# State products of an attention block on quarters and column halves of the array, with compact state and two result banks

## The chip, the cores and the metric

One core of a Trainium2 chip. The metric is the device time of one execution in microseconds, lower is better. All arithmetic is fp32.

## The reference

Attention with decay, in blocks along the sequence, and a mixture of experts on its result:

```python
for b in range(nb):
    intra = einsum('bhic,bhjc->bhij', qb, kb) * Dmask
    intra = einsum('bhij,bhjd->bhid', intra, vb)
    inter = einsum('bhid,bhde->bhie', qb * lam_pow, kv_state)     # query side of the state
    out[:, :, sl] = intra + inter
    kv_state = lam_block * kv_state + einsum('bhsd,bhse->bhde', kb * rev_pow, vb)   # state update
...
for e in range(E):
    out += p[:, e:e+1] * (maximum(x @ w1[e], 0) @ w2[e])
```

There are 4 batches, 8 heads of 64, 768 positions; then 3072 rows of 512 through 4 experts of width 1024. The kernel cuts the attention into 24 chunks of 128 positions, six per batch. The first chunk of a batch has no state to query, the last need not update it. Chunks 0 to 7 run in an opening of some 60 us, the others are strewn among the expert products, which take nearly all the time.

## The kernel before

Heads go in pairs (2hp, 2hp+1), one in each half of the 128 partitions. The state `kv` of a pair is a 128x128 block with two 64x64 blocks on its diagonal and zeros beside them. `half[0]` and `half[1]` are the two halves of the partitions.

```python
def values(n, tags):
    op = bank(tags[0], "op")
    if not first:
        for hp in range(NHP):                       # query side: 4 matmuls on the whole array
            nc.tensor.matmul(out=op[:, hp * C:(hp + 1) * C], lhsT=kv[:, hp], rhs=hc(qs)[:, hp],
                             start=(hp == 0), stop=False, skip_group_check=True)
    for hp in range(NHP):
        for hd in range(2):                         # scores times v: 8 matmuls on column halves
            nc.tensor.matmul(out=op[half[hd], hp * C:(hp + 1) * C], lhsT=vn[:, 2 * hp + hd], ...)
    nc.scalar.copy(out=xT[:, :, c * C:(c + 1) * C], in_=hc(op))
    if not last:
        kp = bank(tags[1], "kvp")
        for hp in range(NHP):                       # state update: 4 matmuls on the whole array
            nc.tensor.matmul(out=hc(kp)[:, hp], lhsT=kn[:, 2 * hp:2 * hp + 2] ..., rhs=vn[:, 2 * hp:2 * hp + 2] ...)
        # later, on VectorE, for each half sl: kv[sl, :, sl] = kv[sl, :, sl] * decay + kpv[sl, :, sl]
```

The score products (64 rows of the contraction, two row halves) are a step of their own, `scores`. Between the steps run `pg` products (first layer, L549 here and L555 after) and `q` products (second layer, L601 and L607).

## Time and profile before

| | before |
|---|---|
| time, median of 4 runs | 1240.24 us (1239.68 to 1241.35) |
| span of the profiled run | 1241.5 us |
| TensorE busy | 1225.3 us |
| VectorE busy | 761.6 us |
| query side and state update, busy | 21.2 and 23.2 us |

TensorE is the bound and the products to be changed are a small part of it. The prediction shows the lines and how they are read. The spacing of starts is the cost of a matmul, not the duration in its row. And a gap of TensorE is printed at the instruction behind it, with what ended it.

### The profile page before, as it was taken

The numbers are of one execution on the slowest core, as the hardware profiler recorded it, in microseconds if no ns is written. First come the engines' busy times: TensorE is split into PE (matmuls) and PEld (weight loads), VectorE is DVE, ScalarE is ACT, GpSimd is POOL, SyncE is SP. The second block draws the span as 40 slices with busy tenths as digits, with TensorE's granted clock in tenths as the row PEclk, the third lists the DMA queues.
The fourth block names the chain that finished last, engine by engine and source line by source line (L and its number), as shares of the span: only waits on it lengthen the run. The fifth ranks groups of instructions, "written<-read, shape, count | busy, mean of one in ns | idle before, by whom it ended". The sixth has DMA issues, their size and how long they took to land.

```text
span 1241.5 us, 16264 instructions
## 1 busy us (share of the span) xinstructions
PE 1225.3 (99%) x6376; PEld 1074.6 (87%) x6376; DVE 761.6 (61%) x1268; ACT 216.9 (17%) x361; POOL 309.1 (25%) x314
## 2 busy tenths in 40 slices
PE   8999999999999999999999999999999999999998
PEld 6888887888888888888888888888888888888887
DVE  5586576577466846745664774764765755755742
ACT  2222111112212211221121120120120220220100
POOL 4520256672382865120000800000110000000001
PEclk9999999999999999999999999999999999999999
DMA  9652679999899699766544864545555454454422
GB/s 226 166 179 86 219 256 347 357 337 312 295 334 323 219 351 354 246 216 208 178 153 153 302 227 168 214 153 217 203 194 216 153 199 183 161 220 154 169 69 84
DMA packets 173277, 273.11 MB, mean 220 GB/s; under 512 B 87440, under 2 KB 120848, under 8 KB 173200
## 3 DMA queue, kind: packets, MB, share of 16 engines
q1 hardware_dynamic: 144384, 212.89, 50.8%
q10 hardware_dynamic: 26704, 53.41, 11.3%
q0 software_dynamic: 2112, 5.77, 1.2%
q8 instruction: 50, 0.82, 0.3%
q14 instruction: 27, 0.22, 0.0%
HBM read 212.39 MB, written 59.64 MB: 219 GB/s over the span
## 4 chain that ended last, share of the span: by engine, by line
PE 90%; DMA 3%; POOL 3%; DVE 2%; issue 0%; ACT 0%; SPq 0%; POOLq 0%; ACTq 0%; DVEq 0%
PE q L601 43%; PE pg L549 34%; PE pM L650 5%; PE sp L378 2%; PE op L405 2%; POOL ops L93 2%; PE kvp L414 2%; PE op L399 1%; DMA w_ops<-ops 1%; PE qp L355 1%; PE kp L355 1%; DMA w2b<-in_moe_w_dram 1%; DVE hS L93 1%; POOL w2o L93 1%; POOL w1o L93 1%; DVE m L93 1%
## 5 line engine op out<-in xcount | busy, mean ns | idle before, releaser
L549 PE MATMUL pg<-xs_in,ws_in 128*128 128x256 f32 x1960 | 472.1, 381 | 3.6 <-ACT m L557 2.5
L549 PEld LDWEIGHTS pg<-xs_in,ws_in 128*128 128x128 f32 x1960 | 371.5, 191 | 55.1 <-ACT m L557 2.9
L601 PE MATMUL q<-w2t,hS 128*128 128x256 f32 x1536 | 361.0, 380 | 0.0
L93 DVE TENSOR_TENSOR m<-pg,m 128x512 f32<-128x512 f32 x410 | 280.2, 689 | 107.2 <-PE pg L549 94.2
L601 PEld LDWEIGHTS q<-w2t,hS 128*128 128x128 f32 x1536 | 291.8, 190 | 39.2
L617 DVE SCALAR_TENSOR_TENSOR acc<-q,gate,acc 128x256 f32<-128x256 f32 x288 | 139.1, 483 | 247.8 <-PE q L601 247.5
L601 PE MATMUL q<-w2t,m 128*128 128x256 f32 x1152 | 270.7, 380 | 0.0
L601 PEld LDWEIGHTS q<-w2t,m 128*128 128x128 f32 x1152 | 219.1, 191 | 29.4
L620 POOL DMA_DIRECT2D out_dram<-acc x44 | 24.1, 548 | 545.9 <-DVE acc L617 545.9
L561 ACT ACTIVATE m<-m 128x512 f32<-128x512 f32 x120 | 75.5, 630 | 357.8 <-DVE m L93 347.2
L93 DVE TENSOR_TENSOR hS<-m,m 128x512 f32<-128x512 f32 x96 | 73.3, 768 | 13.2 <-ACT m L561 13.2
L557 ACT COPY m<-pg 128x512 f32<-128x512 f32 x80 | 46.8, 585 | 170.8 <-PE pg L549 164.3
L93 DVE TENSOR_TENSOR m<-m,m 128x512 f32<-128x512 f32 x96 | 70.5, 739 | 0.0
L503 ACT ACTIVATE m<-m 128x512 f32<-128x512 f32 x48 | 30.3, 630 | 148.7 <-DVE m L93 135.7
L93 POOL TENSOR_TENSOR kn<-kn,s_decay 128x256 f32<-128x256 f32 x40 | 28.2, 724 | 107.7 <-PE kp L355 94.4
L614 DVE TENSOR_SCALAR acc<-q,gate 128x256 f32<-128x256 f32 x48 | 23.2, 482 | 40.5 <-PE q L601 40.4
L650 PE MATMUL pM<-xt,w1o 128*128 128x256 f32 x192 | 43.9, 381 | 1.4 <-DVE xt L93 0.9
L650 PEld LDWEIGHTS pM<-xt,w1o 128*128 128x128 f32 x192 | 36.2, 190 | 7.0 <-DVE xt L93 1.3
L93 DVE TENSOR_TENSOR m<-pM,m 128x512 f32<-128x512 f32 x40 | 27.4, 688 | 22.6 <-PE pM L650 22.4
L93 DVE TENSOR_TENSOR hS<-hS,m 128x512 f32<-128x512 f32 x48 | 35.8, 746 | 0.3
L93 DVE TENSOR_TENSOR st<-sp,s_decay 128x512 f32<-128x512 f32 x48 | 32.1, 682 | 6.2 <-PE sp L378 6.1
L93 POOL TENSOR_TENSOR w2o<-w2b 128x1024 f32<-128x1024 f32 x8 | 19.0, 2379 | 67.8 <-DMA w2b<-in_moe_w_dram 42.2
(65 smaller groups left out, 778.1 us busy)
## 6 DMA issues: line engine op xcount, KB each, us to landing
xs_in<-x_ops SPq DMA_DIRECT2D x70, 896.0 KB, 4.7
ws_in<-w_ops SPq DMA_DIRECT2D x70, 896.0 KB, 6.5
w2t<-w_sums SPq DMA_DIRECT2D x96, 256.0 KB, 6.3
w2t<-in_moe_w_dram SPq DMA_DIRECT2D x72, 256.0 KB, 6.4
w_ops<-ops ACTq DMA_DIRECT2D x28, 512.0 KB, 6.3
x_ops<-ops ACTq DMA_DIRECT2D x21, 512.0 KB, 5.0
w2b<-in_moe_w_dram SPq DMA_DIRECT2D x32, 256.0 KB, 4.8
w_sums<-w2o ACTq DMA_DIRECT2D x16, 512.0 KB, 4.4
```

The lines of the kernel that those rows point to most:

```text
L93: eng.tensor_tensor(out=o, in0=a, in1=b, op=op)
L355: nc.tensor.transpose(out=x[:, hp * C:(hp + 1) * C], in_=y[:, 2 * hp:2 * hp + 2].rearrange("p h d -> p (h d)"), identity=ident[:],)
L378: nc.tensor.matmul(out=sp[hd][:, hp * C:(hp + 1) * C], lhsT=hc(kT)[half[hd], hp], rhs=hc(qT)[half[hd], hp], start=True, stop=True,)
L405: nc.tensor.matmul(out=op[half[hd], hp * C:(hp + 1) * C], lhsT=vn[:, 2 * hp + hd], rhs=hc(st[hd])[:, hp], start=(first and hp == 0), stop= ...
L414: nc.tensor.matmul(out=kpv[:, hp], lhsT=kn[:, 2 * hp:2 * hp + 2].rearrange("p h d -> p (h d)"), rhs=vn[:, 2 * hp:2 * hp + 2].rearrange("p ...
L503: nc.scalar.activation(out=o[:], in_=o[:], func=AF.Relu)
L549: nc.tensor.matmul(out=p[:, j * 256:(j + 1) * 256], lhsT=ws[:, W1_AT[i], j * P:(j + 1) * P], rhs=xs[:, X_AT[i]], start=(fresh and j == 0), ...
L557: nc.scalar.copy(out=new[at][:], in_=p[:])
L561: nc.scalar.activation(out=new[at][:], in_=new[at][:], func=AF.Relu)
L601: nc.tensor.matmul(out=p[:, s * DH:(s + 1) * DH], lhsT=h[A_OF[m]][:, c * 256 + s * P:c * 256 + (s + 1) * P], rhs=fed2[g, e, m][uu][:, c], ...
L617: nc.vector.scalar_tensor_tensor(out=o, in0=x, scalar=w, in1=o, op0=ALU.mult, op1=ALU.add)
L650: nc.tensor.matmul(out=p[:, s * 256:(s + 1) * 256], lhsT=a[c][:, f:f + P], rhs=b[:, c, j * 256:(j + 1) * 256], start=(s == 0 and c == 0), ...
```

## The change

Its intent: multiply no zeros and compute nothing that is thrown away. On the query side each head's 64x64 product takes one quarter of the array, four heads at once. In the state update all 128 positions are summed over, so each head takes a column half (128 rows, 64 columns), two heads at once. For the quarters a head needs its row half and its column half chosen separately. Heads are now numbered 4r + 2a + x: `r` is the half of the rows (and the result bank), `x` the half of the columns. The order of heads in memory changes for q and k, so these come in two loads each. The state is compact, 64 wide. The core of the diff:

```diff
-    op = bank(tags[0], "op")
+    op = [bank(tags[r], "op") for r in range(2)]
+    heads = [(a, r, c) for a in range(2) for r in range(2) for c in range(2)]
     if not first:
-        for hp in range(NHP):
-            matmul(out=op[:, hp * C:(hp + 1) * C], lhsT=kv[:, hp], rhs=hc(qs)[:, hp], ...)
+        for a, r, x in heads:
+            matmul(out=op[r][half[x], a * C:(a + 1) * C], lhsT=kv[half[r], 2 * a + x],
+                   rhs=hc(qs)[half[r], 2 * a + x], start=(a == 0), ...)
 ...
-    kp = bank(tags[1], "kvp")
-    for hp in range(NHP):
-        matmul(out=kpv[:, hp], lhsT=<pair of kn, 128 columns>, rhs=<pair of vn, 128 columns>, ...)
+    kvp = op[1][:, 2 * C:]                      # in the free half of a result bank
+    for ac in range(NHP):
+        for r in range(2):
+            matmul(out=kvp[half[r], ac], lhsT=kn[:, 2 * ac + r], rhs=vn[:, 4 * r + ac], ...)
 ...
-    nc.scalar.copy(out=xT[:, :, ...], in_=hc(op))
+    for r in range(2):
+        nc.scalar.copy(out=xT[:, 2 * r:2 * r + 2, ...], in_=op[r][:, 0:2 * C] ...)
 ...
-    # two halves: kv[sl, :, sl] = kv[sl, :, sl] * decay + kpv[sl, :, sl]
+    # one piece:  kv = kv * decay + kvp
 ...
-    nc.sync.dma_start(out=x, in_=src)                               # q, k: 256 KB
+    for r in range(2):
+        nc.sync.dma_start(out=to[:, :, r], in_=of[:, :, r])         # q, k: 2 x 128 KB
```

GpSimd's decay of k becomes one instruction instead of two.

More of the change, by code (lines that the diff above doesn't have):

```diff
@@ L100, in load @@
         for name in names:
-            x = small(f"{name}n")[:].rearrange("p (h d) -> p h d", d=D)
+            x = small(f"{name}n")
             src = {"q": q, "k": k, "v": v}[name][b, :, c * C:(c + 1) * C, :]
-            nc.sync.dma_start(out=x, in_=src.rearrange("h p d -> p h d"))
-            nat[n, name] = x
+            if name == "v":
+                nc.sync.dma_start(out=x[:].rearrange("p (h d) -> p h d", d=D), in_=src.rearrange("h p d -> p h d"))
+            else:
+                to, of = x[:].rearrange("p (i r d) -> p i r d", r=2, d=D), src.rearrange("(r i) p d -> p i r d", r=2)
+                for r in range(2):
+                    nc.sync.dma_start(out=to[:, :, r], in_=of[:, :, r])
+            nat[n, name] = x[:].rearrange("p (h d) -> p h d", d=D)
     lam_bc = consts.tile([P, H], FP32, name="lam_bc")
@@ L290 @@
     s_decay = consts.tile([P, 2, NHP, C], FP32, name="s_decay")
-    for hd in range(2):
-        for hp in range(NHP):
-            h = 2 * hp + hd
+    for r in range(2):
+        for ac in range(NHP):
+            h = 4 * r + ac
             nc.vector.tensor_tensor_scan(
-                out=s_decay[:, hd, hp], data0=lam_bc[:, h:h + 1].to_broadcast([P, C]), data1=ident[:],
+                out=s_decay[:, r, ac], data0=lam_bc[:, h:h + 1].to_broadcast([P, C]), data1=ident[:],
                 initial=0.0, op0=ALU.mult, op1=ALU.add,
@@ L302 @@
     q_decay = consts.tile([P, NHP, C], FP32, name="q_decay")
-    for hd in range(2):
-        nc.vector.tensor_copy(
-            out=q_decay[half[hd], :, 0], in_=lam_bc[half[hd], :].rearrange("p (hp hd) -> p hd hp", hd=2)[:, hd],
-        )
+    for r in range(2):
+        nc.vector.tensor_copy(out=q_decay[half[r], :, 0], in_=lam_bc[half[r], 4 * r:4 * r + 4])
     m = 1
@@ L313 @@
         m *= 2
-    kv = consts.tile([P, NHP, P], FP32, name="kv")
-    nc.vector.memset(kv[:], 0.0)
+    kv = consts.tile([P, NHP, D], FP32, name="kv")
     probs = consts.tile([P, NTOK // P, E], FP32, name="probs")
@@ L353, in turn @@
         for x, y in ((qp, qn), (kp, kn)):
-            for hp in range(NHP):
+            for ac in range(NHP):
                 nc.tensor.transpose(
-                    out=x[:, hp * C:(hp + 1) * C], in_=y[:, 2 * hp:2 * hp + 2].rearrange("p h d -> p (h d)"),
+                    out=x[:, ac * C:(ac + 1) * C], in_=y[:, 2 * ac:2 * ac + 2].rearrange("p r d -> p (r d)"),
                     identity=ident[:],
@@ L366, in turn @@
         if n % NCH < NCH - 1:
-            for hd in range(2):
-                kd = kn.rearrange("p (hp hd) d -> p hd hp d", hd=2)[:, hd]
-                tt(nc.gpsimd, kd, kd, k_decay[:, hd].unsqueeze(2).to_broadcast([P, NHP, D]), ALU.mult)
+            kd = kn.rearrange("p (ac r) d -> p ac r d", r=2)
+            by = k_decay.rearrange("p r ac -> p ac r").unsqueeze(3)
+            tt(nc.gpsimd, kd, kd, by.to_broadcast([P, NHP, 2, D]), ALU.mult)
     def scores(n, tags):
         qT, kT, _ = turned[n]
-        sp = [bank(tags[hd], "sp") for hd in range(2)]
-        for hp in range(NHP):
-            for hd in range(2):
+        sp = [bank(tags[r], "sp") for r in range(2)]
+        for ac in range(NHP):
+            for r in range(2):
                 nc.tensor.matmul(
-                    out=sp[hd][:, hp * C:(hp + 1) * C], lhsT=hc(kT)[half[hd], hp], rhs=hc(qT)[half[hd], hp],
+                    out=sp[r][:, ac * C:(ac + 1) * C], lhsT=hc(kT)[half[r], ac], rhs=hc(qT)[half[r], ac],
                     start=True, stop=True,
@@ L395, in values @@
         first, last = n % NCH == 0, n % NCH == NCH - 1
-        op = bank(tags[0], "op")
+        op = [bank(tags[r], "op") for r in range(2)]
+        heads = [(a, r, c) for a in range(2) for r in range(2) for c in range(2)]
         if not first:
-            for hp in range(NHP):
+            for a, r, x in heads:
                 nc.tensor.matmul(
-                    out=op[:, hp * C:(hp + 1) * C], lhsT=kv[:, hp], rhs=hc(qs)[:, hp], start=(hp == 0), stop=False,
-                    skip_group_check=True,
-                )
@@ L403, in values @@
-        for hp in range(NHP):
-            for hd in range(2):
-                nc.tensor.matmul(
-                    out=op[half[hd], hp * C:(hp + 1) * C], lhsT=vn[:, 2 * hp + hd], rhs=hc(st[hd])[:, hp],
-                    start=(first and hp == 0), stop=True, skip_group_check=True,
-                )
-        nc.scalar.copy(out=xT[:, :, c * C:(c + 1) * C], in_=hc(op))
-        if not last:
-            kp = bank(tags[1], "kvp")
-            kpv = hc(kp)
-            for hp in range(NHP):
-                nc.tensor.matmul(
-                    out=kpv[:, hp], lhsT=kn[:, 2 * hp:2 * hp + 2].rearrange("p h d -> p (h d)"),
-                    rhs=vn[:, 2 * hp:2 * hp + 2].rearrange("p h d -> p (h d)"), start=True, stop=True,
-                )
-            def state(sl):
+                    out=op[r][half[x], a * C:(a + 1) * C], lhsT=kv[half[r], 2 * a + x], rhs=hc(qs)[half[r], 2 * a + x],
@@ new lines, in values @@
+                    start=(a == 0), stop=False, skip_group_check=True,
+                )
+        for a, r, x in heads:
+            nc.tensor.matmul(
+                out=op[r][half[x], a * C:(a + 1) * C], lhsT=vn[:, 4 * r + 2 * a + x], rhs=hc(st[r])[:, 2 * a + x],
+                start=(first and a == 0), stop=True, skip_group_check=True,
+            )
+        kvp = op[1][:, 2 * C:].rearrange("p (h d) -> p h d", d=D)
+        if not last:
+            for ac in range(NHP):
+                for r in range(2):
+                    nc.tensor.matmul(
+                        out=kvp[half[r], ac], lhsT=kn[:, 2 * ac + r], rhs=vn[:, 4 * r + ac], start=(ac == 0), stop=True,
+                        skip_group_check=True,
+                    )
@@ L420, in state @@
+        for r in range(2):
+            nc.scalar.copy(
+                out=xT[:, 2 * r:2 * r + 2, c * C:(c + 1) * C],
+                in_=op[r][:, 0:2 * C].rearrange("p (a t) -> p a t", t=C),
+            )
+        if not last:
+            def state():
                 if first:
-                    nc.vector.tensor_copy(out=kv[sl, :, sl], in_=kpv[sl, :, sl])
+                    nc.vector.tensor_copy(out=kv[:], in_=kvp)
                 else:
-                    tt(
-                        nc.vector, kv[sl, :, sl], kv[sl, :, sl], q_decay[sl, :, C - 1:C].to_broadcast([D, NHP, D]),
-                        ALU.mult,
-                    )
@@ L427, in state @@
-                    tt(nc.vector, kv[sl, :, sl], kv[sl, :, sl], kpv[sl, :, sl], ALU.add)
-            soon(n, *(lambda sl=sl: state(sl) for sl in half))
+                    tt(nc.vector, kv[:], kv[:], q_decay[:, :, C - 1:C].to_broadcast([P, NHP, D]), ALU.mult)
+                    tt(nc.vector, kv[:], kv[:], kvp, ALU.add)
+            soon(n, state)
     def attention(g):
```

## The prediction

> **What bounds the kernel now.** I read the page first: the busy row and the chain that ended last.
>
> ```profile
> span 1241.5 us, 16264 instructions
> PE 1225.3 (99%) x6376; PEld 1074.6 (87%) x6376; DVE 761.6 (61%) x1268; ACT 216.9 (17%) x361; POOL 309.1 (25%) x314
> PE 90%; DMA 3%; POOL 3%; DVE 2%; issue 0%; ACT 0%; SPq 0%; POOLq 0%; ACTq 0%; DVEq 0%
> ```
>
> TensorE has work for 1225 of 1241 us, and 90% of the chain lies on it. A microsecond taken from TensorE comes off the span, except in the other 10%. The groups by shape then tell how much of it the change touches:
>
> ```profile
> L378 PE MATMUL sp<-qT,kT 64*128 64x128 f32 x384 | 29.7, 298 | 1.3 <-ACT kT L361 1.3
> L405 PE MATMUL op<-st,vn 128*64 128x128 f32 x384 | 26.6, 282 | 0.0
> L414 PE MATMUL kvp<-vn,kn 128*128 128x128 f32 x160 | 23.2, 288 | 0.0
> L399 PE MATMUL op<-qs,kv 128*128 128x128 f32 x160 | 21.2, 276 | 1.1 <-DVE kv L421 1.1
> ```
>
> The state products are L399 and L414, some 20 us each (the busy times include pipeline tails). "128*128" is the array tile: today both use the whole array, although half of what they multiply is zeros (L399) or thrown away (L414). That caps the gain: 40 of 1240 us, if they vanished. L378 and L405 already use halves ("64*128", "128*64"). A mean of 276 ns says little, as matmuls overlap, so I read cost as the distance between starts, from the timeline of TensorE around one chunk:
>
> ```profile
> 610.63 1.68 PE L549 MATMUL pg<-xs_in,ws_in 128*128 128x256 f32 x7
> 612.14 1.05 PE L399 MATMUL op<-qs,kv 128*128 128x128 f32 x8
> 613.12 1.09 PE L405 MATMUL op<-st,vn 128*64 128x128 f32 x16
> 614.15 1.16 PE L414 MATMUL kvp<-vn,kn 128*128 128x128 f32 x8
> 615.14 1.03 PE L601 MATMUL q<-w2t,hS 128*128 128x256 f32 x4
> ```
>
> An fp32 matmul of the program is two records, so x8 is four matmuls. L399 starts at 612.14, L601 at 615.14: the chunk's products take 3.00 us. Single records of 128 columns on the whole array start 0.110 us apart; 8 x 0.110 = 0.88, and L399 takes 0.98. L405 issues 16 records in 1.03: single records show them in pairs, two within 7 ns, pairs 0.110 apart, so the two halves run truly together. Sum: 3 x 0.88 = 2.64, and 0.36 for two changes of tile shape.
>
> Last, the chain between 122 and 220 us, the one long stretch not on TensorE:
>
> ```profile
> 141.48 4.06 DMA w_sums<-w2o
> ...
> 187.75 1.65 POOL kn L93 x2
> 189.40 1.83 POOL ops L93 x2
> ...
> 204.76 8.89 DMA w_ops<-ops
> ...
> 214.67 3.67 PE pg L549 x8
> ```
>
> From 126 to 214 us the weights' sums on GpSimd and their DMAs set the pace; TensorE ends by waiting 2.5 us for them.
>
> **What the Trainium skill says.** "TensorEngine Tiling (Array Packing)", Key Properties: tiles work independently, 64x64 gives four of them, and a change of tiling mode drains TensorE. The trace agrees for halves (pairs 7 ns apart) and shows the drain as the 0.36 us above. Gotcha 1: PSUM Pressure on that page: different row tiles must not use one PSUM bank at once; hence the two result banks here, one per row half. "TensorE: Matmul & The Clock Gate", LDWEIGHTS: load time goes with the columns of the stationary operand, P/1.2 ns; a 64-column load is half a 128-column one. Trace: 138 against 192 ns for the records, which include a fixed part. The same page, Back-to-back issue gap, gives a floor of about 25 ns between matmul starts, or 62 ns where the sequencer decodes in software. The trace has 7 ns inside a pair but never more than two per 110 ns, so it does not show whether four per 110 ns can be sustained.
>
> **The change part by part.**
>
> TensorE, query side (L399): 4 full matmuls become 8 of 64x64 (16 records), ordered so that four neighbours lie on four quarters. With four at once: 16/4 x 0.110 = 0.44 us, from 0.88. State update (L414): 4 full matmuls of 128 columns become 8 column-half matmuls of 64 columns: 8 pairs x 0.055 = 0.44, from 0.88. They use L405's shape and follow it, so that change of shape goes. L405's own work stays 0.88. Changes of shape: full to quarters 0.15, quarters to column halves 0.15, halves to full 0.20; 0.50, from 0.36. Middle chunk: 0.44 + 0.88 + 0.44 + 0.50 = 2.26, from 3.00: 0.74 saved. First chunk of a batch (no L399): 0.44. Last (no L414): 0.44 - 0.15 = 0.29.
>
> There are 24 chunks, 16 middle, 4 first, 4 last. If all counted: 11.8 + 1.8 + 1.2 = 14.8 us. Now where they lie:
>
> - Chunks 0 and 1 finish before the transposes of chunk 4. The load of k for chunk 4 was issued at 19.35 and took 7.4 us, so it landed at 26.75; its transpose ran at 26.90. DMA is above 90% busy there. Whatever is saved before (some 1.5 us) is swallowed by that landing.
> - Chunks 2 to 7: in this part a score product with row halves follows, so one shape change goes entirely and a middle chunk saves 0.93. Chunks 2 to 4: 2.8; chunk 5: 0.3; chunks 6 and 7, up to the first matmul that waits for VectorE at 65.66: about 2.0, since the state update before that wait is two VectorE instructions shorter. Sum 5.1.
> - Chunk 8 (168.8 us) lies inside the GpSimd and DMA chain: its 0.74 is absorbed.
> - Chunks 9 to 23, behind 214 us: 10 middle, 2 first, 3 last: 7.4 + 0.9 + 0.9 = 9.2.
>
> VectorE: the state is compact, 128x256 in place of two 64x256, so 72 instructions become 36. At 0.42 to 0.67 us each 18 us of 762 go. Worth time only where VectorE holds TensorE: before 417.7 and 424.8 us, idle 0.35 + 0.73 us, where the chain passes through four kv instructions (2.2 us). I count 1.0.
>
> ScalarE: the 24 result copies of 128x512 (584 ns) become 48 of 128x256, estimated 370 ns each (fixed part plus half the elements): 4 us more of 217, off the path. The kv update now waits for the second copy, as they share a bank; the background queue hides that after the opening, and in chunk 6 the single kv copy makes up for it. GpSimd: 40 decays of 128x256 become 20 of 128x512, about as long in all. DMA: q and k come in two halves; the runs stay 256 bytes, so packets and bytes stay, 48 issues more. First matmul perhaps 0.3 us later, hidden by the landing above; that landing may slip 0.5.
>
> Sum: 5.1 + 9.2 + 1.0 - 0.5 = 14.8, so 1240 - 15 = 1225 us.
>
> **The rivals.**
>
> (a) Quarters don't run four at once: the records of one fp32 matmul stand one behind the other in program order, and if TensorE looks only one tile ahead, or issue sustains only two starts per 110 ns, L399 stays 0.88 and the 64-column pairs take up to 0.88. Then only shape changes (+0.14 x 16) and VectorE remain: 1238 to 1242. For it: the trace has no denser issue. Against it: in the first 14 us, where all of TensorE's blocks take about twice as long (four transposes 1.09, later 0.60), 16 score records took 2.01 us (7.38 to 9.39), later 1.09; so the array sets that rate, not issue. And pairs start 7 ns apart although the second record of the first tile stands between them in program order. One of the two sides may fall alone: 1231 to 1234.
>
> (b) Supply takes the place: in 200 to 400 us DMA is 92 to 101% busy and the chain before 214 proves that feeding can bind. The tightest weight tile behind 214 landed 2.4 us before use, so a gain of 0.7 per chunk leaves it ahead. If the extra issues slow the queue: 1229 to 1234.
>
> (c) The opening becomes DMA-bound further, with twice as many q and k loads in the same eight rotating completion semaphores: up to 3 us of the 5.1 lost, 1228.
>
> (d) More than expected: wait chains through VectorE shorten elsewhere too, 1219 to 1221.
>
> **Range and chances.** The sum gives 1225, the rivals (b) and (c) pull up by a few us, (a) with perhaps a quarter of the chance by up to 15. Range 1218 to 1236. Faster by over 2% needs under 1215.3, a saving of 25 us, more than all state products could give at fourfold speed: 4%. Slower by over 2% needs 25 us lost on an engine that only gets less work: 2%. Within 2%: 94%.
>
> **What would show it.** Timeline of one middle chunk behind 214 us: query side about 0.59 us from start to start, L405's work 1.03, state update 0.6 to 0.7; the whole 2.2 to 2.3. Records in fours, 110 ns apart. If the query side shows about 1.0, rival (a) holds. The stall before the first product at 214.67 should become longer than 2.5 us by about 0.7, the idles near 417 and 425 should vanish, VectorE's busy time fall to about 744. TensorE idle in the opening near 26 us proves the k landing. The prediction is wrong in kind if TensorE's busy time does not fall by some 12 us, or if it falls and new waits of more than 5 us appear.

## The result, and the profile after

| | before | after |
|---|---|---|
| time, median of 4 runs | 1240.24 us | 1226.18 us (1224.29 to 1227.07) |
| span of the profiled run | 1241.5 | 1225.0 |
| TensorE busy | 1225.3 | 1209.3 |
| VectorE busy | 761.6 | 743.4 |
| ScalarE busy | 216.9 | 219.6 |

The ratio is 0.9884 (95%: 0.9866 to 0.9901). A ratio is the mean time of one kernel's runs over that of the other's of the same rounds, so not quite the ratio of the medians. It is a gain of 1.2%, inside the 2% that counts as the same.

The page of the changed kernel, busy row and chain:

```profile
PE 1209.3 (99%) x6696; PEld 1053.7 (86%) x6696; DVE 743.4 (61%) x1231; ACT 219.6 (18%) x385; POOL 305.5 (25%) x294
PE 92%; DMA 4%; POOL 2%; DVE 1%; ACT 0%; issue 0%; SPq 0%; POOLq 0%; DVEq 0%
```

TensorE issues 320 matmul records more and is busy 16 us less: more, smaller matmuls, several at once. The changed products in the groups by shape:

```profile
L405 PE MATMUL op<-qs,kv 64*64 64x128 f32 x320 | 13.3, 282 | 1.0 <-DVE kv L430 1.0
L418 PE MATMUL op<-vn,kn 128*64 128x64 f32 x320 | 12.7, 222 | 0.0
```

The mean of one query record has even risen, from 276 to 282 ns; the busy time fell from 21.2 to 13.3 us for twice as many. One middle chunk in TensorE's timeline (start, length, as before):

```profile
567.20 0.38 PE L555 MATMUL pg<-xs_in,ws_in 128*128 128x256 f32 x1
567.51 0.67 PE L405 MATMUL op<-qs,kv 64*64 64x128 f32 x16
568.11 1.09 PE L410 MATMUL op<-st,vn 128*64 128x128 f32 x16
569.03 0.64 PE L418 MATMUL op<-vn,kn 128*64 128x64 f32 x16
569.60 1.78 PE L607 MATMUL q<-w2t,hS 128*128 128x256 f32 x7
```

From 567.51 to 569.60 is 2.09 us, where the kernel before needed 3.00. That flatters: the record ahead, at 567.20, keeps TensorE 0.31 us where such a record else takes 0.216, and the first one behind takes 0.320. Part of the changes of shape is hidden in the neighbours. Counted from the last record ahead to the second one behind, less two ordinary ones, a middle chunk costs 3.44 - 0.43 = 3.01 us before and 2.72 - 0.43 = 2.28 after. Single records show the query side as four groups of four starts within 20 ns; the second group comes 160 ns after the first, the others 110 ns apart.

Where it went, by two landmarks that both timelines have. The first opening product (pM) that waits for VectorE started at 65.66 and now at 59.01, 6.65 us earlier; 0.70 of that is its shorter wait. The first product behind the wait for GpSimd and DMA started at 214.67 and now at 207.86, 6.81 earlier. The end came 16.5 earlier. So the opening gave 6.65 us, the stretch up to the wait 0.2, all behind it 9.7.

Before:

```profile
65.66 2.64 PE L650 MATMUL pM<-xt,w1o 128*128 128x256 f32 x11 [0.93 <-DVE xt L93]
214.67 1.65 PE L549 MATMUL pg<-xs_in,ws_in 128*128 128x256 f32 x3 [2.53 <-ACT m L557]
```

After:

```profile
59.01 9.30 PE L656 MATMUL pM<-xt,w1o 128*128 128x256 f32 x42 [0.23 <-DVE xt L93]
207.86 1.74 PE L555 MATMUL pg<-xs_in,ws_in 128*128 128x256 f32 x4 [3.23 <-ACT m L563]
```

The bracket is TensorE's idle time before the instruction: at the second landmark 3.23 us, 2.53 before the change.

### The profile page after: what moved, and what is told of

Read it like the earlier page. It is cut to its first block, busy times and chain, and to the rows that moved or that the text cites. A ratio compares the mean times of both kernels' runs of the same rounds, so it can differ in the third digit from the quotient of the medians.

```text
span 1225.0 us, 16958 instructions
## 1 busy us (share of the span) xinstructions
PE 1209.3 (99%) x6696; PEld 1053.7 (86%) x6696; DVE 743.4 (61%) x1231; ACT 219.6 (18%) x385; POOL 305.5 (25%) x294
## 4 chain that ended last, share of the span: by engine, by line
PE 92%; DMA 4%; POOL 2%; DVE 1%; ACT 0%; issue 0%; SPq 0%; POOLq 0%; DVEq 0%
PE q L607 44%; PE pg L555 34%; PE pM L656 5%; PE sp L382 2%; PE op L410 2%; PE kp L359 1%; PE op L405 1%; DMA w2t<-in_moe_w_dram 1%; PE qp L359 1%; POOL ops L93 1%; DMA w_ops<-w1b 1%; DMA w1b<-in_moe_w_dram 1%; PE op L418 1%; POOL w2o L93 1%; DVE hS L93 1%; DMA w_ops<-ops 0%
## 5 line engine op out<-in xcount | busy, mean ns | idle before, releaser
L93 DVE TENSOR_TENSOR hS<-m,m 128x512 f32<-128x512 f32 x96 | 67.5, 708 | 13.9 <-ACT m L567 13.9
L93 POOL TENSOR_TENSOR kn<-kn,s_decay 128x512 f32<-128x512 f32 x20 | 23.8, 1192 | 103.0 <-PE kp L359 100.8
L423 ACT COPY xT<-op 128x256 f32<-128x256 f32 x48 | 17.1, 373 | 118.6 <-PE op L410 90.9
```

Source lines behind the costliest of these rows:

```text
L93: eng.tensor_tensor(out=o, in0=a, in1=b, op=op)
```

## The experiments

**The state update alone.** Does each half pay by itself, and is it the array that pays? The kernel before, with the new state update only; pairs, loads and block-diagonal state as they were.

```diff
-    for hp in range(NHP):
-        matmul(out=kpv[:, hp], lhsT=<pair of kn>, rhs=<pair of vn>)
+    kpv = kp[:, 0:NHP * D]
+    for hp in range(NHP):
+        for hd in range(2):
+            matmul(out=kpv[half[hd], hp], lhsT=kn[:, 2 * hp + hd], rhs=vn[:, 2 * hp + hd], start=(hp == 0), ...)
```

> The kernel before with the state update alone changed: 8 column-half matmuls of 64 columns in place of 4 on the whole array; query side, loads and block-diagonal state as before. My theory (array time comes off the span): state update 0.56 us from start to start in place of 0.99, and about 0.43 less per chunk behind 214 us (12 chunks, 5.1 us) and 0.6 less in each of the seven of the opening (about 4): saves 8 to 9 us, 1231 to 1232. Rival (the gain of the whole change comes mainly from the shorter VectorE work and the opening's loads, which this run does not have): saves under 3 us, over 1237.

Measured: 1232.24 us, ratio 0.9930 (0.9909 to 0.9951). A chunk in its timeline:

```profile
569.39 1.05 PE L399 MATMUL op<-qs,kv 128*128 128x128 f32 x8
570.37 1.09 PE L405 MATMUL op<-st,vn 128*64 128x128 f32 x16
571.29 0.64 PE L415 MATMUL kvp<-vn,kn 128*64 128x64 f32 x16
571.86 0.91 PE L602 MATMUL q<-w2t,hS 128*128 128x256 f32 x3
```

The query side still takes 0.98 us, the state update 0.57 instead of 0.99, and the block ahead of it 0.92 instead of 1.02, since the shape no longer changes between them. 0.7% of 1240 is 8.7 us, as the theory had it. VectorE's work was not shortened here, so the rival falls.

**The query side alone.** The changed kernel with the state update back on the whole array.

```diff
-    for r in range(2):
-        matmul(out=kvp[half[r], ac], lhsT=kn[:, 2 * ac + r], rhs=vn[:, 4 * r + ac], ...)
+    matmul(out=kvp[ac // 2][:, ac % 2], lhsT=kn[:, 2 * ac:2 * ac + 2], rhs=<heads ac and 4 + ac of vn>, ...)
+    # VectorE reads the diagonal blocks in four pieces
```

> The changed kernel with the state update back on the whole array (4 matmuls of 128 columns, diagonal blocks read out by VectorE in four pieces): quarters for the query side alone. My theory: query block 0.60 us in place of 0.98, with 0.09 more on leaving the full array, so 0.29 less per chunk behind 214 us (13 chunks, 3.8 us) and 2.4 in the opening, state update back at 0.99: saves 5 to 7 us against the kernel before, 1233 to 1235. With the run of the state update alone the two savings should add up to the whole change's 14 to 16. Rival (quarters only pay together with the shared shape of the two column-half blocks): saves under 3.

Measured: 1236.04 us, ratio 0.9955 (0.9937 to 0.9973). By the ratio that is 5.6 us, within the 5 to 7; the time lies above the 1233 to 1235 expected. In its trace the query block takes 0.60 us and the state update 1.00, as before (0.99). By the ratios the two parts add to 8.7 + 5.6 = 14.3 us, and the whole change gives 0.0116 x 1240 = 14.4; that this agrees so well is partly luck, since each ratio is known to some 2.5 us. The traces are sharper. Compared with the kernel before, each chunk behind the wait at 214 us that has the product concerned saves 0.43 us in the first run and 0.29 in the second, and each of the ten that have both saves 0.72 in the changed kernel: block by block, the two parts add.

**The order of issue.** Does TensorE run four at once only because neighbours lie on different quarters?

```diff
-    for a, r, x in heads:
+    for a, r, x in sorted(heads, key=lambda t: (t[1], t[2], t[0])):
```

> The changed kernel with the query matmuls grouped by quarter (four records of one quarter in a row) in place of neighbours on four quarters. Theory A (TensorE starts what it finds for a free quarter anywhere in its queue): records still in fours, query block 0.60 us, time within 1 us of the changed kernel, 1226. Theory B (it looks past only a few waiting records, and the order of issue is what makes fours): fewer at once, query block 0.9 to 1.5 us, 20 chunks of which about 18 count, so 5 to 16 us slower, 1231 to 1242.

Measured: 1227.20 us, ratio 0.9886 (0.9869 to 0.9903). A chunk's query side and its successor:

```profile
569.97 0.69 PE L405 MATMUL op<-qs,kv 64*64 64x128 f32 x16
570.59 1.09 PE L410 MATMUL op<-st,vn 128*64 128x128 f32 x16
```

0.62 us from start to start, 0.02 more than before. Single records still start in fours, now 13 ns apart instead of 7, and the fours 110 ns apart. Four records of one quarter stand in a row in the program, so the first of the fourth quarter has to pass earlier ones that wait; TensorE lets it. (The trace doesn't name the quarter of a record. That each four is one of each quarter follows from the rate, and the spacing of 13 ns shows that the new order did reach TensorE.) Theory A holds, and my rival (a) falls with room to spare.

**The loads in halves.** The kernel before with q and k in two loads each.

```diff
-    nc.sync.dma_start(out=x, in_=src)
+    for hs in (slice(0, 4), slice(4, 8)):
+        nc.sync.dma_start(out=x[:, hs], in_=src[hs])
```

> The kernel before with q and k loaded in two halves each, as the changed kernel does, nothing else. My prediction let the landing of chunk 4's k (26.75 us) swallow what chunks 0 and 1 save; in the changed kernel it landed at 25.16. Theory A (smaller loads land earlier): here too it lands at 25 to 25.5, and the span stays within 2 us of before, since TensorE does not wait there. Theory B (it landed earlier because the changed kernel asks for it earlier, as TensorE frees things sooner): lands at 26.5 to 27 again.

Measured: 1241.08 us, ratio 1.0001 (0.9983 to 1.0018). Chunk 4's k landed at 25.57. Issued at 19.44 and 20.00, no earlier than the whole load of before (19.35), so it was not asked for earlier. From issue to landing a whole load took 7.4 us in two kernels (before and the state update alone), the second half 5.6 here and 4.8 to 5.4 in three others with halves. That speaks for theory A, though 25.57 lies just outside the 25 to 25.5 expected. Theory B isn't excluded as a second part: in the state update alone, with whole loads, k was issued at 18.39, 0.96 us earlier than before, and landed 0.95 earlier, at 25.80. It does not make the landing harmless. Where TensorE comes still earlier or the load later, it waits: in the state update alone 0.41 us for q and 0.27 for k; in the run with the other order of issue, where q landed at 25.43 and k at 26.32, like this:

```profile
25.56 0.63 PE L359 MATMUL qp<-ident,qn 128*128 128x128 f32 x4 [0.54 <-DMA qn<-in_q_dram]
26.41 0.63 PE L359 MATMUL kp<-ident,kn 128*128 128x128 f32 x4 [0.22 <-issue]
```

The changed kernel itself:

```profile
25.20 0.60 PE L359 MATMUL qp<-ident,qn 128*128 128x128 f32 x4
25.64 0.60 PE L359 MATMUL kp<-ident,kn 128*128 128x128 f32 x4
```

No bracket, so no wait. Nor is there one in its second profile. But of the six other profiles with the same code up to here (the two with padding, the two with pieces alone, and the two with the copies on VectorE) all show one, for q, k or both: 0.2 us in two of them, 0.6 to 1.7 in the other four. (I took two loads because versions with one load did not build with this order of heads; no run shows that.)

**Which chunks count.** The query products of one chunk done five times over: 4 x 0.44 us of added TensorE work with the same result, first in chunk 8, ahead of the wait at 208 us, then in chunk 13, behind it.

```diff
-    for a, r, x in heads:
+    for a, r, x in heads * (5 if n == 8 else 1):      # 13 in the second kernel
```

> The changed kernel with the query products of chunk 8 done five times over (same result): 4 x 0.44 = 1.8 us of added TensorE work inside the stretch before the stall at 208 us. My claim is that what chunk 8 saves is absorbed there, so what it costs is absorbed too: the stall falls from 3.2 to about 1.5 us and the first product behind it starts at the same time, 207 to 209; time 1226 plus or minus 1. Rival (the stall only follows TensorE's own pace): everything behind moves by 1.8, 1228.

> The same 1.8 us added in chunk 13 (about 363 us), where I counted savings in full: the first product behind it starts 1.8 us later, and so does the end; time 1228. A difference between this run and that of chunk 8 of about 1.8 us confirms which chunks count. If a wait behind it (the idle at 414 us) takes it up, then 1226 to 1227, and the idle of 1.8 us there shrinks.

Measured: chunk 8: 1226.41 us, ratio 0.9869 (0.9849 to 0.9889); chunk 13: 1230.05 us, ratio 0.9899 (0.9879 to 0.9919). The padding is there in chunk 8, and the wait behind it still is:

```profile
161.87 2.41 PE L405 MATMUL op<-qs,kv 64*64 64x128 f32 x80
164.22 1.09 PE L410 MATMUL op<-st,vn 128*64 128x128 f32 x16
...
208.64 1.13 PE L555 MATMUL pg<-xs_in,ws_in 128*128 128x256 f32 x4 [2.52 <-ACT m L563]
```

1.75 us of work (2.35 in place of 0.60) cost nothing that shows: the ratio is no worse than the changed kernel's 0.9884. Its interval is wider than 1.75 us, so the wait is the better witness: with the padding ahead of it TensorE still stands idle for 2.52 us (I had expected 1.5; the wait ended at 208.64 and not 207.86).

The same work in chunk 13 cost 3.6 us more than in chunk 8 by the medians. That is more than the 1.8 expected, and the two intervals overlap. Its trace shows a wait of 4.83 us at 210.16, ahead of the padding, so not caused by it, and TensorE at half clock for 6.8 us from 208.6 on; in the changed kernel it was 3.4 us. Laid beside the changed kernel's trace, it splits cleanly: the wait ends 2.30 us later, half clock adds 0.90, and across the padding (at 336.73 us, not near 363 as I had written) the distance grows from 3.20 to 4.95. These 1.75 us stay to the end (4.94). So work in chunk 13 counts in full, and the rest of the 3.6 is the wait.

This wait makes much of the difference between runs of one kernel: in five profiles of code that is the same up to there it ended at 206.5, 207.9, 208.4, 210.2 and 210.5 us, and in some a stretch at half clock follows. The mean granted clock of each run points the same way. Of the 21 runs of the kernel before, the twelve at 1.000 took 1238.7 to 1241.7 us, the nine below 1242.0 to 1245.3.

**The idle time at 414 us.** I had expected it to vanish with the shorter state work; it stayed, 1.4 us. VectorE just before its end, in the changed kernel:

```profile
406.68 0.68 DVE L93 TENSOR_TENSOR hS<-m,m 128x512 f32<-128x512 f32 x1
407.28 0.48 DVE L623 SCALAR_TENSOR_TENSOR acc<-q,gate,acc 128x256 f32<-128x256 f32 x1
407.67 0.82 DVE L93 TENSOR_TENSOR hS<-m,m 128x512 f32<-128x512 f32 x1
408.42 1.28 DVE L93 TENSOR_TENSOR m<-pg,m 128x512 f32<-128x512 f32 x2
409.62 2.33 DVE L93 TENSOR_TENSOR hS<-hS,m 128x512 f32<-128x512 f32 x1
```

One shape, one operation, 0.68 and 2.33 us. From 409.05 GpSimd runs a sum of 128x1024 that takes 2.35 us. The Trainium skill, "SBUF — State Buffer", section "SBUF: two separate sides", says that VectorE with two inputs from SBUF (the on-chip memory that holds the tiles) and GpSimd share a pair of ports under a lock held for a whole instruction. The block holds only against a GpSimd instruction that reads SBUF, as this sum does. The trace agrees. Of VectorE's sums of 128x512, the 120 that read a product from the accumulator banks (such as m<-pg) while GpSimd is at a sum take at most 0.694 us. The 73 with both inputs in SBUF beside a GpSimd sum take up to 2.54, and the 235 alone at most 0.693. So cut GpSimd's large sums (four in the program for each group of rows, eight in the trace, 2.35 to 2.81 us):

```diff
-    tt(nc.gpsimd, t[:], a, b, op)                       # 128 x 1024
+    for c in range(2):
+        for s in (slice(0, 256), slice(256, 512)):
+            tt(nc.gpsimd, t[:, c, s], a[:, c, s], b[:, c, s], op)
```

> The changed kernel with GpSimd's four x sums of 128x1024 (2.35 us each) cut into pieces of 128x256. I had predicted that the idle near 414 us goes with the state's VectorE instructions; it stayed (1.4 us). Theory: VectorE's hS sums of 0.7 us take 2.3 there because they wait for the GpSimd instruction running, so shorter ones make VectorE's longest hS 1.4 us or less and the idle at 414 falls under 0.5: 1 to 1.5 us saved, 1225. Rival (VectorE simply has too many instructions there): idle stays at 1.2 or more.

Measured: 1225.04 us, ratio 0.9862 (0.9844 to 0.9880). Its VectorE in the corresponding place:

```profile
405.15 0.68 DVE L93 TENSOR_TENSOR hS<-m,m 128x512 f32<-128x512 f32 x1
405.80 0.48 DVE L625 SCALAR_TENSOR_TENSOR acc<-q,gate,acc 128x256 f32<-128x256 f32 x1
406.20 0.77 DVE L93 TENSOR_TENSOR hS<-m,m 128x512 f32<-128x512 f32 x1
406.89 1.32 DVE L93 TENSOR_TENSOR m<-pg,m 128x512 f32<-128x512 f32 x2
408.13 0.79 DVE L93 TENSOR_TENSOR hS<-hS,m 128x512 f32<-128x512 f32 x1
```

The sum of 2.33 us now takes 0.79, the longest of them in this stretch 1.20, and TensorE has no idle time there: 1.57 us gained at 414. The rival falls: there are as many VectorE instructions as before (1231). But TensorE waits 0.43 us at 486, where the changed kernel does not, and 0.60 of the gain is lost there; what ended that wait the profile doesn't name.

**The wait at 208 us.** TensorE waits there for a ScalarE copy (ACT m). ScalarE's timeline in the changed kernel (ACTq is its sequencer, issuing DMAs):

```profile
204.04 0.33 ACTq L147 DMA_DIRECT2D w_ops<-ops  x1
206.85 0.33 ACTq L148 DMA_DIRECT2D w_ops<-w1b  x1
207.22 0.59 ACT L563 COPY m<-pg 128x512 f32<-128x512 f32 x1 [6.01 <-DMA w_ops<-w1b]
```

The copy stands behind a store that is issued only at 206.85, when earlier stores have landed. So give the copies of that unit's first product to VectorE:

```diff
+    elif old is None and (g, e, m) == (0, 2, "M1"):
+        nc.vector.tensor_copy(out=new[at][:], in_=p[:])
     elif old is None:
         nc.scalar.copy(out=new[at][:], in_=p[:])
```

> The changed kernel with the four M1 copies of the unit behind the stall at 208 us done by VectorE in place of ScalarE. Theory: the stall of 3.2 us is ScalarE standing at the issue of a weight store that waits for its turn, with a copy that TensorE needs behind it in the same queue. Then the stall at 208 goes to under 0.5 us, and the half-clock stretch of 3.4 us after it too: 2 to 5 us saved, 1221 to 1224. Rival (weights or x operands are what is late, the copy only the last of several): a stall of 2 us or more stays, on a DMA landing, within 10 us behind; saves under 1.5.

Measured: 1225.94 us, ratio 0.9866 (0.9849 to 0.9883). The wait at 208 is gone and two others have come, 0.70 us at 217 and this one:

```profile
231.32 1.97 PE L555 MATMUL pg<-xs_in,ws_in 128*128 128x256 f32 x8 [2.15 <-issue]
```

The profile names no releaser, but the weight tile that this product reads landed at 231.23, 10.9 us after its issue. In the changed kernel it was issued 2.15 us earlier, landed at 228.21 and kept nobody waiting. The rival holds in substance, though it said within 10 us and the wait came 23 behind: 3.23 us of waiting became 2.85, and the weights came too late here. Why their load was issued later isn't shown. The half-clock stretch did go: at 250 us this kernel was 1.45 us ahead of the changed one. At the end it was 0.5, mainly for a new wait of 0.66 us at 487.

**A better version?** The changed kernel again, the pieces on GpSimd, and pieces and copies together, on one chip.

> The changed kernel once more, as the base of comparison for the next two on the same chip: 1225 to 1227, ratio to before 0.988.

> The changed kernel with the four x sums on GpSimd in pieces of 128x256, five rounds: the idle of 1.4 us near 414 us is gone for good, so 1 to 1.5 us under the changed kernel of the same call, 1224 to 1225; if the one-look gain was chance, no difference.

> Pieces on GpSimd and the four copies on VectorE together: the copies alone only moved the stall of 208 us to a weight tile landing at 231, so nothing beyond the pieces is expected but the half-clock stretch after the stall, about 1 us: 1223 to 1225.

| kernel | median us | ratio to before (95%) |
|---|---|---|
| changed kernel again | 1227.56 | 0.9887 (0.9869 to 0.9906) |
| pieces on GpSimd | 1224.56 | 0.9860 (0.9844 to 0.9877) |
| pieces and copies | 1225.33 | 0.9864 (0.9843 to 0.9886) |

The pieces were the best, with nearly the same ratio (0.9862 and 0.9860), and both traces have lost the idle at 414. The interval still overlaps that of the changed kernel. The medians differ by 3.0 us, but the traces give some 1.0 (1.6 gained at 414, 0.6 lost near 488), and of the runs at a mean clock of 1.000 the three of the changed kernel have a median of 1225.2, the five with pieces 1224.8. So the idle time is gone, and a gain in the whole time is likely but not shown. The copies add nothing, as expected. The second profile of the changed kernel shows the wait at 208 us with 1.67 in place of 3.23 us, and no half clock: it differs so much from one execution to the next. That the first profile shows 3.23, just the 2.5 plus 0.7 of the prediction, is chance.

## Why the prediction was right, and where not

The time was predicted as 1225 and measured as 1226.2. By its steps:

- *A middle chunk: 2.26 from 3.00.* 2.28 from 3.01. The streaming terms held: fours 110 ns apart for the query side, pairs 58 ns apart for the update (0.055 predicted). The sum of shape changes is 2.28 - 0.44 - 0.88 - 0.44 = 0.52 (0.50 predicted), and single records place it about as I laid it. Full array to quarters: 0.09 in the record ahead and 0.05 between the first two fours, 0.14 (0.15 predicted). Quarters to column halves: 0.11 and 0.05, 0.16 (0.15). Halves to full: 0.10 behind the last pair and 0.10 in the first record on the whole array, 0.20 (0.20). The last 0.02 is the 58 in place of 55 ns.
- *Chunks 0 and 1 are swallowed by k's landing.* This step failed. The landing was not fixed at 26.75, as the step assumes: k landed at 25.16, and the transposes of chunk 4 started 1.26 us earlier (26.46 to 25.20) with no wait. I had even subtracted 0.5 for a later landing. That halves land sooner is what the run with halved loads speaks for; that an earlier request helps too is not excluded. The wait itself exists: it is absent in both profiles of the changed kernel, but other profiles of the same opening show 0.2 to 1.7 us of it, for q or k. So what the step took away whole goes in part, and how much differs from one execution to the next.
- *Chunks 2 to 7 give 5.1.* From chunk 4's transposes to the landmark, 39.20 us became 33.81: 5.4. Chunks 2, 3 and 4 gave 0.94, 0.91 and 0.93 (0.93 predicted), the rest 2.6 (2.3), 0.70 of it at VectorE's wait.
- *Chunk 8 is absorbed.* The padding shows it: 1.75 us more work there still leaves TensorE waiting 2.52 us behind it.
- *Chunks 9 to 23 give 9.2, VectorE's relief 1.0.* Together 9.7 measured. The chunks' own parts are near what was predicted: 10 x 0.72 + 2 x 0.43 + 3 x 0.29 = 8.9. The VectorE term failed: of the two idle times that it was to end, 0.35 us went but the other grew from 0.73 to 1.40, so some 0.3 was lost there and not 1.0 gained. The idle time at 414 is made by VectorE sums stretched by GpSimd's instructions, not by the four state instructions that stood in the chain of before. What made up for it was luck: a wait of a transpose at 558 us is gone (0.43), and the end behind the last matmul is 0.44 shorter. Neither is owed to shorter VectorE work. The first also went in the state update alone, which leaves that work as it was; the second is as short in the run of the kernel before with halved loads.
- *VectorE falls to about 744.* 743.4. *ScalarE copies at 370 ns.* 373.
- *Rival (a)* is refuted by the fours and by the changed order. *Rival (b)* named a stretch, 200 to 400 us, in which TensorE does wait, but it took little more: 3.23 us at 208 where 2.53 stood before. *Rival (c)* did not happen; the halves helped, if anything.

The sum was right partly by balance: 4.6 predicted for the opening against 6.65, 10.2 for the end against 9.7. These are readings of one pair of profiles. The spans of this pair differ by 16.5 us, the medians by 14.1, because the profiled execution of the kernel before took 1243.29 us, 3 us over its median. Another pair, the kernel before with halved loads and the changed kernel's second profile, neither at half clock behind the wait, gives 8.4 for the end. One sum of the prediction is wrong: at fourfold speed the state products, 20 blocks of 0.98 and 20 of 0.99 us, would give 30 us and not less than 25, so that argument does not close off a gain over 2%.

## What to carry to other kernels

Where heads or blocks are half as wide as the array, choose the row half and the column half of each block separately, so that four blocks make four quarters; count what the changes of shape cost and put blocks of one shape side by side. A saving counts only where the engine is really the bound: read landmarks along the timeline and subtract stretches that end in a wait for something else. Before expecting that less work on an engine ends a wait, look whether that engine's instructions are slow there for another reason.

## What the Trainium skill lacked or had wrong

- "TensorEngine Tiling (Array Packing)" says that a change of mode drains TensorE but gives no cost. Here: 0.14 us from the whole array to quarters, 0.16 from quarters to column halves, 0.20 from column halves to the whole array.
- The same page lists 64x64 mode but no measured gain for it; the measured packings of "TensorE: Matmul & The Clock Gate", Part 3, don't include it either. Here: 80 fp32 records of 64x64x128 in a row took 2.35 us, 27 ns each when 0.16 for the change of shape is left out; the whole array took 0.110 us per record.
- "TensorE: Matmul & The Clock Gate", Part 3, says in its list that weight loads overlap running matmuls only where the row groups differ (the paragraph above the list also names a background weight buffer). On column halves, which share all rows, and on the whole array too, most load records start 1 to 2 ns after a matmul's start, and the spacing stays 110 ns.
- The same page's floor of about 25 ns between starts, or 62 with software decoding, does not say that it is for one tile (its Part 3 has about 4 ns between tiles). Here starts on different tiles lie 7 or 13 ns apart; the sustained 27 ns rules out 62, but not 25 on average.
- The same list says that matmuls start and end in program order, without reordering. With four records of each quarter in a row, fours still formed (0.62 us in place of 0.60), so a later matmul on a free quarter starts ahead of an earlier one on a busy quarter, if each four is one of each quarter, as its rate says.
- The same page, Part 1, puts the drop to half clock after an idle window of about 3.4 us, free-running. Here a wait of 2.5 us, too short to fill such a window, was followed by half clock for 3.4 us (before, and with the padding in chunk 8); waits of 3.08 us in the first run with pieces and 3.45 in the run with halved loads were not. So the length of the wait alone does not decide, and what does isn't shown.
- No page found gives the time from issue to landing of half a load beside a whole one when DMA is busy: 4.2 to 5.6 us for the second half of 256 KB (k of chunk 4), 7.4 for the whole.
